# Zero products between the real ones on TensorE, a new order for the index work of slot 0, and small operations spread over more iterations, in a fused attention and two-expert-layer kernel

## The chip, the cores and the metric

The kernel runs on one core of one Trainium2 chip. The metric is the device time of one execution in microseconds (us), the median over the runs shown. The profile is of one execution of its own, with its own time.

## What is computed

The reference is a windowed attention and, behind it, two mixture-of-experts layers. Sizes: batch 4, 8 heads, 576 positions, head size 64; then 2304 tokens of 512 values, 8 experts with 1024 hidden units. One expert is chosen for each token.

```python
scores = (q @ k.T) / sqrt(64)               # heads 0-3: the last 32 positions
scores = where(mask, scores, -1e9)          # heads 4-7: every 4th of the last 128
x = softmax(scores) @ v                     # -> x: [2304, 512]
...
logits = x @ w_gate;  e = argmax(logits)    # layer 1
out[e==i] = gate * sigmoid(x @ w_output_gate)[:, i] * (relu(x @ w1[i]) @ w2[i])
...
logits = x @ w_gate + modality_bias[modality]   # layer 2, on layer 1's output
out[e==i] = gate * (relu(x @ w1[i]) @ w2[i])
```

## The kernel before

The core has TensorE (PE, its weight loads shown as PEld), VectorE (DVE), ScalarE (ACT), GpSimd (POOL) and SyncE (SP, which issues most DMAs). Each engine takes its instructions strictly in the order in which the program issues them (`tc.manual_schedule()`), so the order of the calls in the source is the order on each engine.

**Attention.** There are 16 pairs of heads, n = 0 to 15 (`NPR`). For pair n the stages are: `khi`, `klo`, `qsc`, `qsplit`, `qdup` split q and k into two half-precision parts on ACT, DVE and POOL; `stA(n, g)` (lines 388 to 399) makes the scores of group g (three groups) on PE and takes their row maxima on DVE; `stM` (from line 401) turns the maxima into a small bias on POOL (six operations, lines 415 to 420; the last pair's on DVE); `stMT` (line 430) transposes it on PE and ACT copies it out; `stB` (lines 443 to 446) makes the transposed scores on PE and their exponential on ACT; `stC(n, h)` (line 459) multiplies by v on PE, and behind h = 1 DVE normalises in three operations (lines 463 to 466); `stH` and `stZ` (474, 481) split the result into two parts on ACT and POOL (DVE for the last two pairs) and write it to `x_dram` through SP; `stX` (514, 521) transposes the last pairs' x on PE; `stR` (530, 531) makes the router's logits `lg1`. The function `iteration(n)` runs these for different pairs in the order of the list `ORDER`:

```python
ORDER = 'C0 T A0 H DV S0 Q0 Z A1 MT Q1 P0 S1 C1 K0 W L0 B0 X0 A2 D X1 K1 DW R S2 L1 B1 B2 P1 DQ MS'.split()
STEP = {'A': (stA, 1), 'B': (stB, 0), 'C': (stC, -1), 'X': (stX, -2), ...}
```

The number beside a stage is its offset: A works on pair n+1, C on n-1. At the place `W`, which lies behind C1 and ahead of L0, and at the start of the iteration, generators are stepped: `first_expert` (`fes`, from iteration 8) finds from the first 512 tokens the expert that will have the first slots; its result `gi` is read by SP at `DW` of iteration 10, where the loads of that expert's weights begin (two pieces of 512 KB in each of iterations 10 to 13). At iteration 3 `slot_consts` (12 small DVE operations, lines 153 to 164) and `token_values` (one, line 170) run in one go. `tail()` writes out by hand the order of what is left behind iteration 14, with `his` and `los` (splitting the loaded weights into a high part on ACT, line 102, and a low part on DVE, line 107) and `fs` (the steps of `first_slots`) between the stages.

**Expert layers.** Tokens are sorted by expert and worked through in slots of 128. `first_slots` picks the tokens of slots 0 and 1 (`KA` = 2) by itself: maxima, ranks by two products on PE (250, 251), one-hot rows `A` (line 230), products that give the token numbers (275), the numbers as integers (278), two gathers by POOL from `x_dram` (280), and a transposition on PE for each slot (`turn`, 542, 543). `sort` does the same for all tokens: step 1 maxima and one-hot (724 to 739), step 2 products (743 to 746), step 3 places (750 to 824), step 4 the one-hot matrix `A` (230), step 5 products (834), step 6 the integer indices (838), the gathers of slots 2 to 4 (903), a `table` of the experts (787 to 815) and the load of slot 3's weights by `start.weights(KE)` (line 94, on SP, 8 pieces), step 7 and 8 the gates (848 to 875), step 9 their products (880).

`moe` runs slot after slot. A slot is: `mm1(0)` and `mm1(1)` (line 940, 48 products of 128 columns each, `ph`), each followed by `hsplit` (ReLU and high part on ACT, line 950; low part `hl` on DVE, line 951), then 24 products of 512 columns into `py` (line 1012). Slots 0 to 2 use the weights loaded during attention, slot 3 the first that the table names; `first_splits(FIRST[i])` splits a quarter of these on ACT and DVE. Work is put into a slot by `at(s, k, ...)`: k = 0 start, 8 and 1 in `mm1(0)` behind 8 and 32 products, 2 behind it, 3 ahead of `mm1(1)`, 4 in it behind 32, 5 behind the second `hsplit`, 9, 6 and 10 behind 4, 12 and 20 products into `py`, 7 the end. `post.out` scales a slot's result on ACT and DVE (1155, 1156), `post.turn` transposes it (1174, 1175), `post.router` makes layer 2's logits (1183, 1192) in a PSUM tile `plg`. Slots from `NMIN` = 18 on stand in nested `tc.If(nsl > s)` (line 1041), with a branch hint for PE and DVE (`HINT`). Layer 2 runs through the same code with `so2`, `start2` and its own list of `at` (lines 1297 to 1312); its last slot of layer 1 is finished inside its slot 0 (`post1.out(None, ...)`, 1151 to 1153).

## Time and profile before

| | us |
|---|---|
| three runs | 639.43, 640.17, 644.14 |
| median | 640.17 |
| the profiled execution, its own time | 638.38 |
| its span, first to last instruction | 636.6 |
| PE busy | 589.1 (93% of the span) |
| DVE, ACT, POOL busy | 359.9, 272.8, 196.1 |
| attention with its tail, to the first product of slot 0 | 0 to 150.6 |
| layer 1, layer 2 | 150.6 to 419, 419.9 to 627.7 |

A row of the timeline gives the start and the length in us, the engine, the line, the operation, the tile written and the tiles read with their sizes, and how many instructions the row stands for. In brackets stands how long the engine had been idle, and whose work ended that. The granted clock is the share of 2.4 GHz that TensorE was given: 1.00 is 2.4 GHz, 0.50 is 1.2 GHz.

### The profile page before, as it was taken

What the parts mean: (1) busy time and instruction counts of PE and PEld (TensorE: products, weight loads), DVE (VectorE), ACT (ScalarE), POOL (GpSimd) and SP (SyncE); (2) the same over time, 40 slices, a digit from 0 to 9 for tenths busy, and PEclk for the clock granted to TensorE, in tenths of its full rate; (3) what the DMA queues carried; (4) which work ended last, traced back from release to release, by engine and by line L of the source; (5) the groups of instructions that cost most, each with busy time, mean ns of one, the idle gap of its engine ahead of it and who ended that gap; (6) DMA issues with size and microseconds to landing.
All of it is one profiled execution on the core that took longest, in us unless ns stands there. A gap on an engine that the chain in (4) does not pass through costs nothing. (4 is left out here: it accounts for less than half of the span.)

```text
span 636.6 us, 19375 instructions
## 1 busy us (share of the span) xinstructions
PE 589.1 (93%) x7380; PEld 456.1 (72%) x7380; DVE 359.9 (57%) x657; ACT 272.8 (43%) x370; POOL 196.1 (31%) x307
## 2 busy tenths in 40 slices
PE   3888889977999999999999999989999999999994
PEld 2868778867668677687776777856777777777772
DVE  6798898888889327944859732247530101013560
ACT  5677767773294126823538411110632111114550
POOL 2567767613151310111110610002654221212120
PEclk9799989975999999999999999999999999999998
DMA  8766668972499856996968683301994423233921
GB/s 290 243 191 194 211 198 273 293 167 72 146 357 368 226 117 180 378 243 151 266 198 221 169 153 65 69 21 36 324 323 121 99 60 93 63 91 114 300 56 37
DMA packets 100864, 114.15 MB, mean 179 GB/s; under 512 B 64399, under 2 KB 69263, under 8 KB 100752
## 3 DMA queue, kind: packets, MB, share of 16 engines
q1 hardware_dynamic: 95072, 94.89, 52.5%
q0 software_dynamic: 5280, 17.13, 9.1%
q8 instruction: 59, 0.97, 0.6%
q10 hardware_dynamic: 400, 0.72, 0.3%
q14 instruction: 53, 0.43, 0.2%
HBM read 209.13 MB, written 18.22 MB: 357 GB/s over the span
## 5 line engine op out<-in xcount | busy, mean ns | idle before, releaser
L940 PEld LDWEIGHTS <-wb 128*128 128x128 f16 x4032 | 229.7, 98 | 7.3 <-issue 1.5
L940 PE MATMUL ph<-xT,wb 128*128 128x128 f16 x3648 | 210.5, 219 | 1.1 <-ACT xT L919 1.1
L951 DVE SCALAR_TENSOR_TENSOR hl<-ph,hh 128x512 f16<-128x512 f32 x84 | 57.7, 689 | 162.8 <-ACTq L959 152.8
L1012 PE MATMUL py<-wb,hh 128*128 128x512 f16 x608 | 137.8, 379 | 0.0
L950 ACT ACTIVATE hh<-ph 128x512 f16<-128x512 f32 x84 | 50.2, 597 | 147.7 <-PE ph L940 147.3
L1012 PEld LDWEIGHTS <-hh 128*128 128x128 f16 x672 | 63.6, 98 | 68.0 <-ACT hh L950 0.3
L107 DVE SCALAR_TENSOR_TENSOR wb<-raw,wb 128x1024 f16<-128x1024 f32 (+1 forms) x80 | 104.7, 1346 | 12.7 <-ACT wb L102 11.3
L102 ACT ACTIVATE wb<-raw 128x1024 f16<-128x1024 f32 (+1 forms) x80 | 87.2, 1135 | 8.2 <-issue 2.8
L1012 PE MATMUL py<-wb,hl 128*128 128x512 f16 x304 | 72.0, 379 | 0.4 <-issue 0.4
L1012 PEld LDWEIGHTS <-hl 128*128 128x128 f16 x336 | 32.9, 98 | 40.2 <-issue 0.7
L1286 POOL DMA_INDIRECT out<-y,idx x16 | 16.2, 1010 | 98.9 <-ACTq L959 80.8
L459 PE MATMUL po<-v,pT 128*96 128x65 f32 x384 | 40.7, 258 | 0.1
L459 PEld LDWEIGHTS po<-v,pT 128*96 128x96 f32 x384 | 37.6, 174 | 0.2 <-DVE xh L466 0.2
L398 PE MATMUL ps<-kk,qs 128*96 128x128 f16 x192 | 30.0, 229 | 4.5 <-DVE qs L382 2.2
L398 PE MATMUL ps<-kk,ql 128*96 128x128 f16 x192 | 30.1, 230 | 4.2 <-DVE ql L376 4.2
L1285 ACT ACTIVATE y<-py,gsb 128x512 f32<-128x512 f32 x16 | 11.0, 687 | 52.3 <-PE py L1012 52.3
L399 DVE TENSOR_REDUCE M<-ps 96x4 f32<-96x512 f32 x48 | 31.6, 681 | 2.6 <-PE ps L398 2.0
L903 POOL DMA_INDIRECT xg<-x_dram,idxaa x23 | 24.4, 1061 | 27.6 <-DMA xT<-xg 18.0
L398 PEld LDWEIGHTS <-ql 128*96 128x96 f16 x192 | 23.5, 130 | 12.5 <-DVE ql L376 5.9
L446 ACT ACTIVATE pT<-pst 128x384 f32<-128x384 f32 x48 | 23.5, 489 | 20.4 <-PE pst L445 19.7
L443 PE MATMUL pst<-mt,msel 128*128 128x96 bf16 x192 | 29.9, 216 | 2.4 <-ACT mt L432 2.4
L398 PEld LDWEIGHTS <-qs 128*96 128x96 f16 x192 | 23.9, 130 | 8.8 <-issue 3.2
(407 smaller groups left out, 726.2 us busy)
## 6 DMA issues: line engine op xcount, KB each, us to landing
raw<-in_w1a SPq DMA_DIRECT2D x95, 512.0 KB
raw<-in_w2a SPq DMA_DIRECT2D x92, 512.0 KB
raw<-in_w1b SPq DMA_DIRECT2D x75, 512.0 KB
raw<-in_w2b SPq DMA_DIRECT2D x72, 512.0 KB
qk<-in_qk SPq DMA_DIRECT2D x16, 608.0 KB
v<-in_vw SPq DMA_DIRECT2D x16, 390.0 KB
y_dram<-y SPq DMA_DIRECT2D x11, 260.0 KB
y_dram<-lotmp SPq DMA_DIRECT2D x10, 260.0 KB
```

The costliest lines, as they stand in the source:

```text
L102: nc.scalar.activation(wb[:, 0, s], raw[:, s], AF.Copy, scale=SW)
L107: nc.vector.scalar_tensor_tensor(out=wb[:, 1, s], in0=raw[:, s], scalar=SW, in1=wb[:, 0, s], op0=ALU.mult, op1=ALU.subtract)
L398: nc.tensor.matmul(ps[:, j, :], q[:, h, QT * i:QT * i + QT], kk[:, h, QT * i:QT * i + 128], start=False, stop=w == 1 and j == 3, skip_grou ...
L399: nc.vector.tensor_reduce(out=Ms[n][:, 4 * g:4 * g + 4], in_=ps, axis=AX.X, op=ALU.max)
L443: nc.tensor.matmul(ps[:, j, :], msel[:, typ, j, :], mt[:, g, :], start=j == 0, stop=False, skip_group_check=True)
L446: nc.scalar.activation(pTs[n][:, 4 * g:4 * g + 4, :], ps, AF.Exp, scale=0.125 / (SQK * SQK))
L459: nc.tensor.matmul(po[:, h, i, :], pT[:, NQ * h + i, :], v[:, h, i, :], start=True, stop=True)
L903: nc.gpsimd.indirect_dma_start(t, None, src, bass.IndirectOffsetOnAxis(start.idx[:, s:s + 1], 0))
L940: nc.tensor.matmul(ph[:, j, :], w[:, c, fs], xT[:, parts[c + i], :], start=k == 0, stop=k == 47, skip_group_check=True)
L950: nc.scalar.activation(hs, ph, AF.Relu)
L951: nc.vector.scalar_tensor_tensor(out=hl[:, 4 * g:4 * g + 4, :], in0=ph, scalar=0.0, in1=hs, op0=ALU.max, op1=ALU.subtract)
L1012: nc.tensor.matmul(to, a, w, start=k == 0, stop=k == len(ops) - 1)
```

## The change

Zero products: a helper `warm` multiplies the zero tile `zt` with itself, 512 columns at a time, into a PSUM tile that nobody reads. It is called at the head (14 at the start, then 7, 6, 2 and 2) and at nine places of `tail()` (29 products in all, six of them inside `stX`). `slot_consts` is cut into four parts that run in iterations 0 (two), 1 and 2, `token_values` moves to `W` of iteration 3. `first_expert` gets more steps, so that `gi` comes at `W` of iteration 10 instead of 9, and one of its operations moves to POOL. In the tail, the last pair's `stC(b, 1)` comes ahead of `stX(a, 1)`, and its normalisation behind the last index step of `first_slots`. The sort of layer 1 runs at other hooks, the first splits' last quarter one hook later, layer 2's indices and gathers five hooks earlier than its table. One router product gets another PSUM tile and an earlier place, and DVE no longer gets branch hints.

```diff
@@ -37,7 +37,6 @@
 NSP = 28
-HINT = [mybir.EngineType.PE, mybir.EngineType.DVE]
 TOK0 = 1536.0
@@ -153,12 +152,15 @@
         v.tensor_scalar(si, si, 1, None, op0=ALU.logical_shift_right)
+        yield
         v.tensor_copy(s_odd, so)
...
         v.tensor_scalar(s_even, s_odd, -1.0, 1.0, op0=ALU.mult, op1=ALU.add)
+        yield
         v.tensor_tensor(s_even, s_even, s_half, op=ALU.mult)
...
         v.tensor_scalar(s_half, s_half, KA - 1.0, None, op0=ALU.add)
+        yield
         v.tensor_scalar(s_two, iota_t, 2.0, None, op0=ALU.mult)
@@ -183,14 +185,21 @@
         mx, eq, mi, me, cnt = T("mx", [P, n]), T("eq", sh), T("mi", [P, n]), T("me", [P, E]), T("cnt", [P, E], F16)
+        t = gp if nm == "a" else v
         v.tensor_reduce(out=mx, in_=lg0, axis=AX.X, op=ALU.max)
         v.tensor_tensor(eq, lg0, mx.unsqueeze(2).to_broadcast(sh), op=ALU.is_equal)
-        v.tensor_tensor(eq, eq, desc.unsqueeze(1).to_broadcast(sh), op=ALU.mult)
+        t.tensor_tensor(eq, eq, desc.unsqueeze(1).to_broadcast(sh), op=ALU.mult)
+        if nm == "a":
+            yield
         v.tensor_reduce(out=mi, in_=eq, axis=AX.X, op=ALU.max)
         v.tensor_tensor(eq, eq, mi.unsqueeze(2).to_broadcast(sh), op=ALU.is_equal)
+        if nm == "a":
+            yield
         v.tensor_reduce(out=me, in_=eq.rearrange("p t e -> p e t"), axis=AX.X, op=ALU.add)
...
         yield
+        if nm == "a":
+            yield
         pm = psum()
@@ -199,7 +208,8 @@
         v.tensor_reduce(out=m, in_=me, axis=AX.X, op=ALU.max)
-        yield
+        if nm != "a":
+            yield
@@ -385,6 +395,12 @@
+        WP = (14, 7, 6, 2, 2)
+
+        def warm(ps, k):
+            for i in range(k):
+                nc.tensor.matmul(ps, zt[:, 0:P], zt[:, 0:512], start=True, stop=True)
+
         def stA(n, g):
@@ -392,6 +408,8 @@
             nc.tensor.matmul(ps, identb[:QT, :QT], mS[kind][:, 4 * g:4 * g + 4, :], start=True, stop=False, skip_group_check=True)
+            if g == 0 and n < 2:
+                warm(wps, WP[1 + n])
             for j in range(4):
@@ -425,6 +443,8 @@
                 return
+            if n == 0:
+                warm(wps, WP[3])
             pm = ps_x.tile([P, 3, QT], BF16, name="pm", tag="px")
@@ -434,6 +454,8 @@
             kk, mt = kks[n], mts[n]
+            if g == 0 and n == 0:
+                warm(wps, WP[4])
             if g == 0:
@@ -457,8 +479,14 @@
                 nc.tensor.matmul(po[:, h, i, :], pT[:, NQ * h + i, :], v[:, h, i, :], start=True, stop=True)
-            if h == 0:
+            if h == 0 or n == NPR - 1:
                 return
+            normalise(n)
+
+        def normalise(n):
+            b, hp = divmod(n, 4)
+            xh = x_half[b, hp // 2]
+            po = pos[n][:, :, 0:65 * NQ].rearrange("q h (i c) -> q h i c", c=65)
             rc = ap2.tile([QT, 2, NQ, 1], F32, name="rc")
@@ -502,7 +530,7 @@
-        def stX(n, g):
+        def stX(n, g, wpt=None):
             if n // 2 in FL['dt']:
@@ -510,6 +538,8 @@
             for w in range(2):
+                if w and wpt is not None:
+                    warm(wpt, 3)
                 for i in range(3):
@@ -562,6 +592,7 @@
             a, b = NPR - 2, NPR - 1
+            wpt = ps_s.tile([P, 512], F32, name="wpt", tag="ps")
             his(2, 3)
@@ -570,6 +601,7 @@
             stZ(b - 2)
+            warm(wpt, 6)
             stB(b, 0)
@@ -585,20 +617,27 @@
             stC(b, 0)
+            warm(wpt, 3)
             fs()
-            stX(a, 0)
-            stX(a, 1)
+            stX(a, 0, wpt)
             fs()
             stC(b, 1)
+            warm(wpt, 2)
+            stX(a, 1)
+            warm(wpt, 2)
             fs()
+            fs()
+            normalise(b)
             stH(b)
-            fs()
             stR(a - 2)
+            warm(wpt, 3)
             stR(b - 2)
...
             los(4)
-            stX(b, 0)
+            warm(wpt, 2)
+            stX(b, 0, wpt)
             stX(b, 1)
+            warm(wpt, 5)
             stR(a)
@@ -621,12 +660,16 @@
                 nc.gpsimd.tensor_copy(midf, midt[:, :, 0])
-                slot_consts()
-                token_values()
+            if n == 0:
+                next(scs)
             if n >= fe_:
...
                 if o == 'W':
+                    if 0 <= n < 3:
+                        next(scs, None)
+                    if n == 3:
+                        token_values()
                     if n >= fe_:
@@ -663,6 +706,9 @@
         actx.enter_context(tc.manual_schedule())
+        scs = slot_consts()
+        wps = ps_v.tile([P, 2, 512], F32, name="wps", tag="po")[:, 0, :]
+        warm(wps, WP[0])
         for n in range(-4, NPR - 1):
@@ -840,6 +886,7 @@
             start.gather(i)
+        yield
         table()
@@ -976,7 +1023,7 @@
             if NMIN - 1 <= s < NSLOT - 1:
-                tc.mark_branch_hint_location(f"{start.name}{s + 1}", hint=nsl > s + 1, engines=HINT)
+                tc.mark_branch_hint_location(f"{start.name}{s + 1}", hint=nsl > s + 1, engines=PE)
             if s >= KE:
@@ -1002,6 +1049,8 @@
                 post.turn(s - 1)
+            if s == NMIN - 1:
+                post.router(s - 2, "pw")
             hook(5)
@@ -1013,8 +1062,6 @@
                     hook(9)
-                    if s == NMIN - 1:
-                        post.router(s - 2)
                 if k == 12:
@@ -1174,8 +1221,8 @@
-        def router(self, s):
-            pl = pp.tile([P, E], F32, name="plg", tag="plg")
+        def router(self, s, tag="plg"):
+            pl = pp.tile([P, E], F32, name=tag, tag=tag)
             yT = self.yT[0 if s is None else s % 2]
@@ -1213,10 +1260,9 @@
     at(0, 0, run(so1), lambda: lo_piece(wbuf[0], 12))
-    at(0, 1, run(so1, 2))
-    at(0, 2, run(fss))
-    at(0, 5, run(so1), lambda: lo_piece(wbuf[0], 14))
-    at(0, 10, run(so1, 2))
+    at(0, 3, run(so1), lambda: lo_piece(wbuf[0], 14))
+    at(0, 5, run(so1, 2), run(fss))
+    at(1, 1, run(so1, 3))
     at(1, 3, run(so1), start1.consts)
@@ -1225,11 +1271,10 @@
     at(2, 3, lambda: start1.first_splits(FIRST[2]))
-    at(2, 5, lambda: start1.first_splits(FIRST[3]))
     for i in range(NSLOT - NMIN):
...
     at(2, 5, first_out(post1, start1, 0))
-    at(2, 6, first_out(post1, start1, 1))
+    at(2, 6, first_out(post1, start1, 1), lambda: start1.first_splits(FIRST[3]))
     at(2, 7, lambda: post1.turn(0), lambda: post1.turn(1, "pw"), lambda: start1.part(KE + 1, *EARLY))
@@ -1289,7 +1334,7 @@
-        def router(self, s):
+        def router(self, s, tag=None):
             pass
@@ -1300,8 +1345,9 @@
     at(0, 7, run(so2, 2))
-    at(1, 9, run(so2, 2))
-    at(1, 7, lambda: start2.turned(KA))
+    at(1, 4, run(so2, 2))
+    at(1, 9, run(so2))
+    at(1, 10, lambda: start2.turned(KA))
     at(2, 2, lambda: start2.turned(KA + 1))
```

## Rows read from the trace of the kernel before

**Rows 1.** The page, part 2: granted clock, 40 slices, in tenths

```profile
PEclk9799989975999999999999999999999999999998
```

**Rows 2.** Windows; length, PE PEld DVE ACT POOL busy, clock, DMA share, GB/s

```profile
16.30:23.20 6.90, 5.93 (x61) 5.42 (x59) 4.40 (x7) 3.32 (x6) 3.61 (x7) 0.51 0.85 268
...
139.30:156.20 16.90, 12.76 (x165) 12.20 (x165) 13.44 (x36) 5.38 (x5) 4.65 (x12) 0.50 0.31 85
156.20:630.00 473.80, 465.49 (x5601) 344.63 (x5598) 229.84 (x397) 169.51 (x227) 108.86 (x154) 1.00 0.60 169
```

**Rows 3.** Timeline, DVE, line 463, five of sixteen; idle time in brackets

```profile
33.39 0.17 DVE L463 TENSOR_SCALAR rc<-po 96x12 f32<-96x12 f32 x1 [0.98 <-PE po L459]
...
42.58 0.16 DVE L463 TENSOR_SCALAR rc<-po 96x12 f32<-96x12 f32 x1
...
71.16 0.17 DVE L463 TENSOR_SCALAR rc<-po 96x12 f32<-96x12 f32 x1 [1.10 <-PE po L459]
...
81.49 0.16 DVE L463 TENSOR_SCALAR rc<-po 96x12 f32<-96x12 f32 x1
...
88.70 0.17 DVE L463 TENSOR_SCALAR rc<-po 96x12 f32<-96x12 f32 x1 [0.42 <-PE po L459]
```

**Rows 4.** Timeline, PE, DVE and POOL, attention's head

```profile
6.97 0.59 PE L394 MATMUL ps<-mS,identb 96*96 96x512 bf16 x1 [6.97 <-DMA mS<-in_cbs]
...
20.43 0.69 DVE L399 TENSOR_REDUCE M<-ps 96x4 f32<-96x512 f32 x1 [0.56 <-PE ps L398]
...
23.76 0.19 POOL L420 CAST mb<-r 96x12 bf16<-96x12 f32 x1
...
25.04 0.29 PE L430 MATMUL pm<-identb,mb 96*128 96x96 bf16 x3
```

**Rows 5.** Timeline, DVE and PE, first-expert work of iteration 8

```profile
77.07 1.63 DVE L188 TENSOR_TENSOR fe_eqa<-fe_eqa,cft 128x32 f32<-128x32 f32 x1
...
80.44 0.18 PE L195 MATMUL pfe<-fe_cnta,c16t 128*128 128x8 f16 x1 [2.13 <-DVE fe_cnta L192]
```

**Rows 6.** Timeline, DVE and PE, attention's tail, start of slot 0

```profile
140.29 1.02 DVE L230 TENSOR_TENSOR fs_A<-c16t,fs_fp 128x1664 f16<-128x1664 f16 x1
142.65 0.17 DVE L463 TENSOR_SCALAR rc<-po 96x12 f32<-96x12 f32 x1 [1.34 <-PE po L459]
...
150.98 0.30 DVE L724 TENSOR_REDUCE mxa<-lg 128x18 f32<-128x144 f32 x1 [0.85 <-DMA x_dram<-x]
...
150.56 3.57 PE L940 MATMUL ph<-xsA,wb 128*128 128x128 f16 x32 [0.71 <-ACT xsA L543]
```

**Rows 7.** Timeline, DVE, SP, ACT and PE, slots 0 to 3

```profile
162.22 1.21 DVE L107 SCALAR_TENSOR_TENSOR wb<-raw,wb 128x1024 f16<-128x1024 f32 x1
164.24 0.18 DVE L838 TENSOR_SCALAR idxaa<-pidx 128x27 int32<-128x27 f32 x1 [0.80 <-PE pidx L834]
...
168.71 1.98 SPq L94 DMA_DIRECT2D raw<-in_w1a  x4
...
181.14 0.61 ACT L950 ACTIVATE hh<-ph 128x512 f16<-128x512 f32 x1
...
182.82 3.62 PE L1012 MATMUL py<-wb,hh 128*128 128x512 f16 x16
...
189.67 0.40 PE L1174 MATMUL pyt<-identh,y 128*128 128x128 f16 x4 [0.70 <-DVE y L1156]
...
190.65 2.84 PE L940 MATMUL ph<-xT,wb 128*128 128x128 f16 x48
```

**Rows 8.** Timeline of PE and DVE, and line 1041's branches, both expert stages

```profile
362.14 0.44 PE L1183 MATMUL plg<-wr2h,yT 128*128 128x8 f16 x12 [0.86 <-DVE lg L1192]
...
422.40 0.75 DVE L1152 SCALAR_TENSOR_TENSOR y<-py,prg,y 128x512 f16<-128x512 f32 x1 [3.07 <-issue]
...
L1041 DVEq COMPARE_BRANCH  x10: 43/50/88, 362.6 to 625.8; - x10
...
446.56 2.84 PE L940 MATMUL ph<-xT,wb 128*128 128x128 f16 x48 [1.10 <-ACT xT L919]
```

## The prediction

> **What bounds the kernel now.** I read the granted clock first, over the whole span and then in windows. In the page's line of slices the reader is to see that the clock is below full only in the first 160 us (each slice is 15.9 us long) [rows 1]. The windows give the size: from 16.3 to 23.2 us the clock is 0.51 and PE works 5.93 us; from 139.3 to 156.2 us it is 0.50; behind that it is 1.00 to the end, and PE is busy for 465.5 of 473.8 us [rows 2]. So from the middle of slot 0 on the kernel is a full PE at full clock: whatever brings PE's stream forward there reaches the end one for one, and nothing else does.
>
> Second, the attention by the start of the normalisations on DVE. One iteration takes 88.70 - 81.49 = 7.21 us, but two take 42.58 - 33.39 = 9.19 and 81.49 - 71.16 = 10.33 us [rows 3]. The reader is to see that in normal iterations DVE waits for PE's `po` ahead of the normalisation (0.42 to 1.10 us), and in the two long ones it doesn't [rows 3]: there DVE itself is late, with one-off work.
>
> Third, single rows of the timeline for the head, the tail, slots 0 to 3 and the places behind them where PE waits.
>
> **Head.** Behind the clock's fall at 16.3 us DVE waits 0.56 us for the scores of pair 1, so pair 1's maxima, and POOL's bias that follows from them, come 0.56 us late. The bias is ready at 23.76 + 0.19 = 23.95, but PE transposes it only at 25.04 with no idle time: another 1.09 us [rows 4]. At full clock both go: 0.56 + 1.09 = 1.65 us. More than half of PE's 5.93 us [rows 2], 3.0, can't be had, and nothing if the clock falls in spite of the zeros: 0 to 3.0, and I take 1.65.
>
> The price of a zero product of 512 columns is that of a product into `py`, 3.62 / 16 = 0.23 us [rows 7], and twice that at half clock. PE's first real product waits until 6.97 us for its mask [rows 4]; 14 zeros cost 3.2 us at full and 6.3 us at half clock and are hidden by that wait. The other 17 stand ahead of products that wait for DVE, POOL or ACT; without that cover they would cost 17 x 0.23 = 3.9 us. I take nothing, with 1 us for the range.
>
> **Iterations 3 and 8.** The excess is 9.19 - 7.21 = 1.98 and 10.33 - 7.21 = 3.12, together 5.1 us. In iteration 8 the chain is seen on PE, which waits 2.13 us for the product of `first_expert` [rows 5]; the new steps put this product two iterations' worth of calls later, behind data that is long ready.
>
> What comes instead: of the cut operations, those stepped at the start of an iteration lie ahead of DVE's wait for `po`, and that wait hides them. Those stepped at `W` lie between the normalisation and the second half of the next split and maxima, and this stretch is on the loop (normalise, split, maxima, bias on POOL, transpose, `po`, normalise). At `W` stand three operations in iteration 1, three in 2, one in 3, two in 8 and four in 10 (`m` and the three ahead of it): 13. One such small operation takes 0.17 us [rows 3], some 0.2 with its gap: 13 x 0.2 = 2.6 us, if all are on the path. What is left is 5.1 - 2.6 = 2.5 us. Best is 5.1, if all 13 are hidden; worst, if two of them are blocked for 1.63 us each as the one in iteration 8 was [rows 5], 2.5 - 3.3 = -0.8.
>
> The multiplication at 77.07 takes 1.63 us on 32 elements, where a small one takes 0.17 [rows 5, 3]: something held it. The Trainium skill, SBUF — State Buffer, section "Who interferes with whom", states that a VectorE instruction with two SBUF inputs and a GpSimd instruction that reads SBUF exclude each other for their whole length. The trace agrees with such a block by this length. By the rule alone every moved operation with two SBUF inputs that meets POOL's split work would be held again, and the gain here would be nearer to the -0.8 than to the 2.5.
>
> SP reads `gi` ahead of the first weight loads, and q, k and v loads are queued behind that. `gi` now comes at `W` of the same iteration. No row prices this wait: between 0 and one iteration's excess as seen in iteration 8, 3.1 us; I take 0, since SP's place `DW` is behind `W`, and keep 1 us of it in the range.
>
> **Tail.** The one-hot matrix of slots 0 and 1 is ready at 140.29 + 1.02 = 141.31; DVE then waits 1.34 us for `po` and normalises at 142.65 [rows 6]. With `stC(b, 1)` ahead of `stX(a, 1)` that wait is gone; next comes the index (13 small products, some 0.45 us after the 0.44 of twelve in rows 8, and itself, 0.2), and the normalisation starts at about 142.05, 0.6 us earlier. What follows (split, write to `x_dram`, logits) moves with it. Sort's first operation at 150.98 waits for that write [rows 6], so DVE starts slot 0 at 150.4, again 0.6 earlier. PE reaches slot 0 at 150.56 behind ACT's copy of the turned tokens [rows 6]; the index no longer lies behind the normalisation, so the gather is issued some 2 us earlier, the copies ahead of it come 0.6 earlier, and eight transpositions at full clock (four take 0.40 [rows 7]) save another 0.4: about 149.5, 1.05 earlier. The 29 zeros (6.7 us at full clock) stand in front of products that wait; up to 1 us of them may show.
>
> **Slots 0 to 2.** PE's work up to 156.2 us at half clock [rows 2] would give back half of 156.2 - 150.56, 2.8 us. Does it arrive? DVE works without a gap from 150.98 to 162.22 + 1.21 = 163.43 [rows 6, 7]: sort, two low parts of weights, two `hl`. The new order puts all of that ahead of the index products, and lets the second `hl` wait some 0.65 us for PE: the list ends at 163.43 - 0.6 + 0.65 = 163.5. Before, the last low part lay behind the one-hot matrix, and the index came at 164.24 [rows 7]. So the index, the gathers, the table and the load of slot 3's weights at 168.71 stay within 0.5 us where they were. In slot 2 ACT splits those weights as they land and only then does `hh`, at 181.14 [rows 7]; PE's products into `py` started at 182.82 because PE was there no earlier. Now PE is there 3 us earlier and waits for `hh`: start at 181.14 + 0.61 + 0.3 = 182.05, 0.8 earlier. From there `out` ahead of the last quarter's split takes away the 0.70 us wait ahead of slot 3 [rows 7]. Slot 3 starts 0.8 + 0.7 = 1.5 us earlier than 190.65. Bounds: all of PE's own gain, 1.05 + 2.8 + 0.7 = 4.6; or, if the index comes 1 us later than before, 0.5. The clock's gain in slot 0 is thus mostly handed on to a wait for `hh`.
>
> **Behind that.** In slot 17 PE waits 0.86 us for DVE to free `plg` [rows 8]; with `pw` I take 0.85 (0 to 0.86). In layer 2 PE waits 1.10 us for the turned tokens of slot 2 [rows 8]; indices and gathers come 16 products of 128 columns and 4 of 512 earlier, 16 x 0.06 + 4 x 0.23 = 1.9 us [rows 7]; I take 0.8 (0 to 1.1), as the turned tokens then wait for their place in PE's stream.
>
> **Sum.** 1.65 + 2.5 + 1.5 + 0.85 + 0.8 = 7.3 us off the profiled execution's 638.38 (span 636.6): 631.1. The runs' median, 640.17, is 1.8 above this execution, and the lowest run, 639.43, 1.0 above. With the lowest run's offset the forecast is **632.1**.
>
> **Rivals.**
> 1. *PE's gain arrives whole in slots 0 to 3*, since ACT meets landed weights: 4.6 instead of 1.5, 629.0. For it: PE is at half clock there. Against: `hh` at 181.14 follows the splits. Chance 0.15.
> 2. *The clock isn't held*: the zeros are fewer than the waits. Then 1.65 is lost, and zeros cost 0.45 each where they show, 1 us: 634.8. For it: between the real products of the tail PE waits for copies. Chance 0.12.
> 3. *The index of the first expert comes too late*: loads behind SP's read slip, later weight pieces land later, and 3 us are given back: 635.1. For it: SP is one queue. Against: the later pieces are issued iterations later anyway. Chance 0.13.
> 4. *Slower: DVE's branches without hints.* At the change of layers DVE has 3.07 us in which the profile shows nothing it waits for, with a hint; line 1041 has 10 branches on DVE [rows 8]. If each, unhinted, costs such a stop, the ceiling is 30.7 us. DVE has cover in these slots; the case decides at 7.3 / 10 = 0.73 us uncovered for each. At half of each uncovered, 15.4 - 7.3 = 8 over before: 648.3. Against: ACT and POOL pass the same line unhinted. Chance 0.05. The Trainium skill, Runtime: NRT & Kernel Launch, section "Instruction fetch mechanics", states that a taken branch to code outside the fetched pages stops the engine for a fetch. The 3.07 us fit it, even with a hint; no row here shows an unhinted DVE.
>
> **How the numbers follow.** The forecast has 0.55, the rivals 0.45. The range: up to rivals 2 and 3 with their zeros' and SP's us, 637.0; down to rival 1 with three quarters of what iterations 3 and 8 could give beyond 2.5 us, 627.0. One per cent, about what can be told from no change, is 633.8. Four fifths of the forecast's chance, rival 1 and a little of 2 and 3 lie below: 0.62. Rival 4 is 0.05, 0.33 is between.
>
> **What would show it.** Right: clock 1.00 from about 9 us; normalisations 7.2 to 7.8 us apart throughout; first product of slot 0 some 5 us earlier; `idxaa` 14 us or more behind it; in slot 2 PE waits for `hh`; no wait for `plg`. Wrong: a clock of 0.5 in the tail; a normalisation 9 us behind the last; PE without a wait in slot 2; DVE idle for over 3 us in gated slots with PE behind it.

## The result and the profile after

The changed kernel takes 632.62 us (median of four runs, 631.73 to 633.55) beside 640.36 us for the kernel before in the same session (639.43 to 644.14): a ratio of 0.9872, 95% interval 0.9844 to 0.9900. A second session on another chip gave 633.27 beside 640.96 us, 0.9887 (0.9867 to 0.9906). The forecast was 632.1 us. The total agrees to half a microsecond; its parts do not all agree, and that is what this section and the experiments are about.

The page of the changed kernel, part 2, shows one of the first ten slices with the clock below full, where the kernel before has four [rows 1] (the last slice, where the work ends, is below full in both):

```profile
PEclk9999998999999999999999999999999999999998
```

The windows (columns as in rows 2) show where this is: the head, the tail and the first 10 us of slot 0 run at the full clock, and the only stretch at half clock ahead of the last product is a new one, at 98 us.

```profile
16.30:23.20 6.90, 6.32 (x86) 4.84 (x84) 6.35 (x13) 4.70 (x7) 4.09 (x11) 1.00 0.87 270
98.00:101.00 3.00, 3.00 (x26) 2.77 (x26) 1.33 (x3) 1.89 (x3) 2.70 (x3) 0.50 1.03 356
...
139.00:148.00 9.00, 6.50 (x101) 4.44 (x100) 7.12 (x13) 3.28 (x3) 3.13 (x12) 1.00 0.42 126
148.00:158.00 10.00, 10.00 (x115) 7.17 (x113) 8.39 (x26) 2.10 (x3) 1.41 (x5) 1.00 0.01 2
```

The normalisations on DVE answer to rows 3. Each row's start is to be compared with the row above it.

```profile
32.05 0.17 DVE L491 TENSOR_SCALAR rc<-po 96x12 f32<-96x12 f32 x1 [0.98 <-PE po L481]
39.37 0.17 DVE L491 TENSOR_SCALAR rc<-po 96x12 f32<-96x12 f32 x1 [1.10 <-PE po L481]
...
68.14 0.17 DVE L491 TENSOR_SCALAR rc<-po 96x12 f32<-96x12 f32 x1 [1.10 <-PE po L481]
75.32 0.17 DVE L491 TENSOR_SCALAR rc<-po 96x12 f32<-96x12 f32 x1
83.09 0.17 DVE L491 TENSOR_SCALAR rc<-po 96x12 f32<-96x12 f32 x1 [0.76 <-PE po L481]
90.39 0.17 DVE L491 TENSOR_SCALAR rc<-po 96x12 f32<-96x12 f32 x1 [0.48 <-PE po L481]
99.60 0.17 DVE L491 TENSOR_SCALAR rc<-po 96x12 f32<-96x12 f32 x1 [2.02 <-PE po L481]
```

The stretches of 9.19 and 10.33 us [rows 3] are gone: 39.37 - 32.05 = 7.32 and 75.32 - 68.14 = 7.18. What follows iteration 8's normalisation takes 7.77, and what follows iteration 10's takes 99.60 - 90.39 = 9.21. (In the experiments "iteration n" is counted like that, from its own normalisation to the next one.) The rows of DVE, POOL and PE behind 90.39 show the chain of that long one:

```profile
91.73 0.15 DVE L207 TENSOR_REDUCE fe_m0a<-pfe 128x1 f32<-128x8 f32 x1
92.51 0.79 DVE L366 SCALAR_TENSOR_TENSOR kk<-qk,kk 64x608 f16<-64x608 f32 x1
94.62 0.64 POOL L220 TENSOR_TENSOR fe_oa<-fe_oa,fe_ua 128x8 f32<-128x8 f32 x1
95.23 0.86 POOL L433 TENSOR_SCALAR r<-M 96x12 f32<-96x12 f32 x1
97.50 0.30 PE L450 MATMUL pm<-identb,mb 96*128 96x96 bf16 x3 [1.10 <-POOL mb L438]
```

The four small DVE operations of `m` push the split `kk` back by 92.51 - 91.73 = 0.78 us; POOL's five operations with the result end at 94.62 + 0.64 = 95.26, and only then comes the bias; PE waits 1.10 for it, and the clock falls.

The tail, on PE, DVE and POOL, and PE's first product of slot 0:

```profile
139.14 0.52 PE L560 MATMUL pl<-wr1h,xT 128*128 128x16 f16 x15
139.42 0.23 DVE L561 TENSOR_TENSOR lg<-pl,lg 128x80 f32<-128x80 f32 x1
141.34 0.24 DVE L561 TENSOR_TENSOR lg<-pl,lg 128x80 f32<-128x80 f32 x1 [1.69 <-remote]
...
140.94 0.33 POOL L291 TENSOR_SCALAR ea_cons<-fs_r 128x13 f32<-128x13 f32 x1
...
142.50 0.56 PE L544 MATMUL px<-identh,x 96*128 96x96 f16 x9 [1.13 <-DVE x L509]
146.69 0.49 PE L987 MATMUL ph<-xsA,wb 128*128 128x128 f16 x6 [0.74 <-ACT xsA L573]
```

DVE stands for 1.69 us between two additions of logits; `remote` says that the view names no instruction that ended this wait. The second addition reads what PE's products at 139.14 write, and those end, as modelled, at 139.66. The trace also records when semaphores go up: the one of PE that this addition waits for goes up at 141.32, 0.02 us ahead of DVE's start. In layer2_old, a run without the stop, the same semaphore goes up at 138.77, 0.02 us behind the end of these products. So DVE waited for PE's signal, and the signal came 1.65 us late. The paragraph on pace below and the run cons_first come back to it. The split behind the stop comes late, and PE waits 1.13.

Slots 0 to 2 and the places behind them (DVE, SP, PE, ACT), to be held against rows 7 and 8:

```profile
160.40 0.18 DVE L884 TENSOR_SCALAR idxaa<-pidx 128x27 int32<-128x27 f32 x1 [0.48 <-PE pidx L880]
165.19 1.71 SPq L93 DMA_DIRECT2D raw<-in_w1a  x4
183.05 1.02 PE L1061 MATMUL py<-wb,hl 128*128 128x512 f16 x4 [0.71 <-POOL y L1196]
...
351.06 0.45 PE L1230 MATMUL pw<-wr2h,yT 128*128 128x8 f16 x12
415.14 0.75 DVE L1199 SCALAR_TENSOR_TENSOR y<-py,prg,y 128x512 f16<-128x512 f32 x1 [1.29 <-ACT y L1198]
438.97 1.22 PE L987 MATMUL ph<-xT,wb 128*128 128x128 f16 x19 [0.24 <-ACT xT L966]
455.17 1.91 ACT L101 ACTIVATE wb<-raw 128x2048 f16<-128x2048 f32 x1 [1.88 <-DMA raw<-in_w2b]
458.48 1.90 PE L1061 MATMUL py<-wb,hh 128*128 128x512 f16 x8 [1.67 <-ACTq L1006]
```

The index comes 160.40 - 146.69 = 13.71 us behind the first product of slot 0, as before (164.24 - 150.56 = 13.68). The wait of 0.86 us for `plg` is gone, and so is DVE's stop of 3.07 us with no wait shown. In layer 2 the wait ahead of slot 2 falls from 1.10 to 0.24, and a new one of 1.67 us stands in slot 3, behind weights that landed late. In slot 2 of layer 1 PE now stops 0.71 us ahead of the last four products into `py`, where it also loads the slot count; 0.42 stood there before.

By stretches, from the starts of such rows (us). Normalisations are counted by pair, so pair 13's is the 14th. "Same pace" is explained below; it is the changed kernel but for two small POOL operations in the tail (the run cons_first).

| stretch | before | after, gain | second profile, gain | same pace, gain | forecast |
|---|---|---|---|---|---|
| start to first normalisation | 26.40 | 1.74 | 1.55 | 1.87 | 1.65 |
| to pair 13's normalisation | 98.81 | 2.13 | 3.05 | 3.07 | 2.5 |
| to slot 0 | 25.35 | 0.00 | 0.02 | 0.35 | 1.05 |
| slot 0 to slot 4 | 51.71 | 1.14 | 0.66 | 0.28 | 0.45 |
| slot 4 to layer 2 | 217.59 | 0.53 | 0.11 | 1.08 | 0.85 |
| layer 2 to the last product | 207.82 | -0.70 | -0.19 | 2.20 | 0.8 |
| sum | 627.68 | 4.84 | 5.20 | 8.85 | 7.3 |

The two profiles of the changed kernel show 5 us, the medians 7.7. The profile of before seems to stem from a chip of a quicker pace (its chip isn't known): its gated slots in layer 2 take 10.54 us each, as in the kernels profiled on the chip where before's medians were 638.35 and 638.22 us, while both profiles of the changed kernel have slots of 10.5 to 11.1 and stand beside medians of 640.4 and 641.0. The slower pace goes with PE's signals: in both profiles of the changed kernel, and in the other four of chips of this pace, 35 to 39 of PE's some 507 signals come late or aren't found beside the end of their product, in before and in the seven profiles of the quicker chip 1 to 3. The stop in the tail is one of these. At its own pace, the profiles of m_now, layer2_old and cons_first, which differ little from the changed kernel, end 7.4, 8.5 and 8.9 us earlier.

### The profile page after: what moved, and what is told of

The parts are those of the page before. It is cut to its first block, busy times and chain, and to the rows that moved or that the text cites. A ratio compares the mean times of both kernels' runs of the same rounds, so it can differ in the third digit from the quotient of the medians.

```text
span 631.8 us, 19474 instructions
## 1 busy us (share of the span) xinstructions
PE 595.4 (94%) x7440; PEld 451.0 (71%) x7440; DVE 356.0 (56%) x656; ACT 273.1 (43%) x370; POOL 193.5 (31%) x308
## 5 line engine op out<-in xcount | busy, mean ns | idle before, releaser
L987 PEld LDWEIGHTS <-wb 128*128 128x128 f16 x4032 | 227.4, 98 | 7.9 <-issue 1.4
L101 ACT ACTIVATE wb<-raw 128x1024 f16<-128x1024 f32 (+1 forms) x80 | 87.5, 1135 | 13.8 <-DMA raw<-in_w2a 3.1
L481 PE MATMUL po<-v,pT 128*96 128x65 f32 x384 | 39.1, 252 | 0.6 <-PE pst L467 0.6
L481 PEld LDWEIGHTS po<-v,pT 128*96 128x96 f32 x384 | 35.8, 167 | 1.4 <-issue 0.7
L950 POOL DMA_INDIRECT xg<-x_dram,idxaa x23 | 26.0, 1131 | 26.0 <-DMA xT<-xg 18.0
L416 PE MATMUL ps<-kk,ql 128*96 128x128 f16 x192 | 28.6, 222 | 4.4 <-DVE ql L386 4.3
L416 PE MATMUL ps<-kk,qs 128*96 128x128 f16 x192 | 28.6, 222 | 3.9 <-DVE qs L392 2.7
L416 PEld LDWEIGHTS <-ql 128*96 128x96 f16 x192 | 22.2, 124 | 11.2 <-DVE ql L386 6.3
L1239 DVE SCALAR_TENSOR_TENSOR lg<-plg,lg 128x8 f32<-128x8 f32 x21 | 3.5, 165 | 45.3 <-PE plg L1230 44.7
L465 PE MATMUL pst<-mt,msel 128*128 128x96 bf16 x192 | 27.5, 207 | 0.6 <-ACT mt L452 0.6
```

The costliest lines, as they stand in the source:

```text
L101: nc.scalar.activation(wb[:, 0, s], raw[:, s], AF.Copy, scale=SW)
L416: nc.tensor.matmul(ps[:, j, :], q[:, h, QT * i:QT * i + QT], kk[:, h, QT * i:QT * i + 128], start=False, stop=w == 1 and j == 3, skip_grou ...
L465: nc.tensor.matmul(ps[:, j, :], msel[:, typ, j, :], mt[:, g, :], start=j == 0, stop=False, skip_group_check=True)
L481: nc.tensor.matmul(po[:, h, i, :], pT[:, NQ * h + i, :], v[:, h, i, :], start=True, stop=True)
L950: nc.gpsimd.indirect_dma_start(t, None, src, bass.IndirectOffsetOnAxis(start.idx[:, s:s + 1], 0))
L987: nc.tensor.matmul(ph[:, j, :], w[:, c, fs], xT[:, parts[c + i], :], start=k == 0, stop=k == 47, skip_group_check=True)
```

## The experiments

Each run gives a ratio to the kernel before on its own chip, and one profile.

**The kernel again.** No edit.

> The changed kernel once more, unchanged. Theory: two places of its first profiled execution are chance and not the kernel's: the 9.21 us of iteration 10 with the clock at 0.5 behind it, and the 1.69 us that DVE waited ahead of the logits in the tail. In a second profile iteration 10 takes 8.5 us, slot 0 starts near 144.6 instead of 146.69, and the time against the kernel before is 0.987 to 0.988. Rival: both belong to the change; they are there again, and slot 0 starts near 146.7.

0.9887 (0.9867 to 0.9906). Iteration 10 took 8.49 us, without a fall of the clock, so 0.7 of the 9.21 was chance. The stop in the tail was there again, so that half of the theory falls. It came back in all four profiles of this chip, each time with PE's signal 1.6 to 1.7 us behind the modelled end of its products:

```profile
138.69 0.23 DVE L561 TENSOR_TENSOR lg<-pl,lg 128x80 f32<-128x80 f32 x1
140.58 0.24 DVE L561 TENSOR_TENSOR lg<-pl,lg 128x80 f32<-128x80 f32 x1 [1.66 <-remote]
...
140.23 0.32 POOL L291 TENSOR_SCALAR ea_cons<-fs_r 128x13 f32<-128x13 f32 x1
```

**Without the zeros.**

```diff
-            for i in range(k):
+            for i in range(0):
                 nc.tensor.matmul(ps, zt[:, 0:P], zt[:, 0:512], start=True, stop=True)
```

> All products of zeros are left out of the changed kernel (they only write a scratch bank, so nothing that is computed goes missing). Theory, each part pays in its own place: the clock falls again in iterations 0 and 1 of the attention and the 1.74 us of the head go; in the tail PE runs at half clock, but DVE and ACT set the end there, so the stretch from the normalisation of iteration 13 to the first product of slot 0 stays at its 17.15 us within 0.5; slot 0 is slower by some 3 us at half clock, of which about two thirds were handed on to later waits anyway. Sum 1.7 + 1.3 = 3.0 us: 635.6. Rival A, the clock is held by the other changes: 632.6 and a clock of 1.00 behind 9 us. Rival B, all that slot 0 gained reaches the end: 1.7 + 3.2 = 4.9 us, 637.5.

0.9947 (0.9928 to 0.9966): 634.59 beside 638.35 us, so the changed kernel's gain halves. Windows of this run, tail and slot 0:

```profile
139.00:148.00 9.00, 5.03 (x98) 4.47 (x99) 7.60 (x15) 3.95 (x4) 4.99 (x12) 0.61 0.44 124
148.00:158.00 10.00, 10.00 (x118) 8.54 (x117) 6.81 (x18) 2.10 (x3) 0.11 (x1) 0.84 0.01 2
```

Against layer2_old, on the same chip: the first normalisation comes 26.03 - 24.76 = 1.3 us later, the stretch from pair 13's normalisation to slot 0 takes 25.28 instead of 24.23, and slot 0 to slot 4 takes 53.50 instead of 51.51. At slot 4 the loss is 201.10 - 196.19 = 4.9 us. That is rival B: what slot 0 gains by the clock arrives at slot 4, and of the 4.9 us the medians of this chip show 4.3 to 4.5 (634.59 beside 630.07 for layer2_old and 630.32 for cons_first).

**The zeros alone,** in the kernel before.

```diff
+        wps = ps_v.tile([P, 2, 512], F32, name="wps", tag="po")[:, 0, :]
+        warm(wps, WP[0])
         for n in range(-4, NPR - 1):
...
             stZ(b - 2)
+            warm(wpt, 6)
             stB(b, 0)
```

> The kernel before with the products of zeros alone, at the same places of head and tail, nothing else changed. Theory: with the old order of slots 0 and 1 the clock's gain there is handed on (the changed kernel with that order back took 51.1 us from slot 0 to slot 4, the kernel before 51.7 with half clock), so the zeros are worth the head's 1.7, about 1.0 in the tail and 0.6 in slots 0 to 3: 3.3 us, a ratio of 0.995. Rival: the clock is worth the same 4.9 to 5.8 us at slot 4 that the changed kernel loses without its zeros: 0.992.

0.9973 (0.9957 to 0.9990): less than either expected, 1.7 us in the medians of 12 runs. The profile is the fastest of them (634.55 us) and shows the expected terms: head 26.40 - 24.61 = 1.79, tail 25.35 - 24.21 = 1.14, slots 0 to 3 51.71 - 50.98 = 0.73. The twelve runs' mean clocks go from 0.984 to 0.995 (0.988 to 0.997 in the nine of the changed kernel), and the slowest runs are among those of the lowest clocks: the zeros don't hold the clock in every execution. How much of what is missing from the expected 3.3 us this explains isn't shown.

**Order of slots 0 to 2 put back.**

```diff
-    at(0, 3, run(so1), lambda: lo_piece(wbuf[0], 14))
-    at(0, 5, run(so1, 2), run(fss))
-    at(1, 1, run(so1, 3))
+    at(0, 1, run(so1, 2))
+    at(0, 2, run(fss))
+    at(0, 5, run(so1), lambda: lo_piece(wbuf[0], 14))
+    at(0, 10, run(so1, 3))
...
-    at(2, 6, first_out(post1, start1, 1), lambda: start1.first_splits(FIRST[3]))
+    at(2, 6, first_out(post1, start1, 1))
```

> In the changed kernel the order of the index work in slots 0 and 1 and the place of the last quarter's split in slot 2 are put back. Theory of the prediction: the index, the gathers and slot 3's weights hang on DVE's list, which is as long in either order, so the index comes 13.7 us behind the start of slot 0 again, and only the wait of 0.70 us ahead of slot 3 returns: 0.7 us slower than the changed kernel. Rival: the new order is what lets slots 0 and 1 use the full clock (DVE's hl no longer stands behind index work), and slot 1 starts 1 us or more later without it: 1.7 us slower or more.

0.9914 (0.9894 to 0.9933), 635.25 beside 633.27 us for after_again, with intervals that overlap. The profile, the fastest of its six runs, shows no loss: slot 0 to slot 4 takes 197.45 - 146.37 = 51.08 us, 51.05 in after_again. Slot 0 is 2.0 us longer, and slots 1 to 3 are 1.3, 0.2 and 0.5 us shorter. Taken together for slots 0 to 3 (us):

| | half clock in the first 3.6 to 5.6 us of slot 0 | full clock |
|---|---|---|
| old order | 51.71 (before) | 50.98, 51.08 |
| new order | 53.50 (no_zeros) | 50.57 to 51.51 (nine profiles, without best_e, whose slot 1 is edited) |

The new order doesn't pay by itself, and at half clock it costs 1.8 us; it ties the index to PE, since `hl` of slot 0 now stands ahead of it on DVE: the index comes 13.72 us behind the start of slot 0 in after_again and 15.42 in no_zeros. The expected 13.7 us for the old order is missed, too: there the index came at 12.49, and nothing of that reached slot 4. That the median of slots_old is 2 us longer isn't explained by its profile and stays open.

**One-off work put back** (`slot_consts`, `token_values` and `first_expert` in one go).

```diff
-        t = gp if nm == "a" else v
+        t = v
...
-            if n == 0:
-                next(scs)
...
+                list(scs)
+                token_values()
```

> In the changed kernel the constants of the slots, the values of the tokens and the first expert's chain are put back as before, in one go in iterations 3 and 8. Theory: iteration 3 loses 1.5 us and iteration 8 some 3.0, and iteration 10, which in the changed kernel takes 9.21 us with four small operations behind the normalisation, returns to 7.2: 4.5 - 2.0 = 2.5 us net, 635.1, with the first product of slot 0 later by as much. Rival: iteration 10 is long for another reason (the read of the first expert's index by SP, the loads behind it) and stays at 9.2: 4.5 us net, 637.1.

0.9927 (0.9908 to 0.9945). The long stretches are back with 9.17 and 10.32 us, and iteration 10 takes 7.24: the theory. From the first normalisation to pair 13's it takes 98.75 - 95.69 = 3.06 us longer than layer2_old. A further 1.1 us of this run's profile were lost at 136 to 140 us, where the clock was 0.68.

**DVE's branch hints put back.**

```diff
-                tc.mark_branch_hint_location(f"{start.name}{s + 1}", hint=nsl > s + 1, engines=PE)
+                tc.mark_branch_hint_location(f"{start.name}{s + 1}", hint=nsl > s + 1, engines=[mybir.EngineType.PE, mybir.EngineType.DVE])
```

> The branch hints of DVE are put back into the changed kernel, nothing else. Theory: the hint made the stop of 3.07 us on DVE at the change of layers, with no wait shown; it comes back, PE waits 1.17 us again behind it in slot 0 of layer 2, and the slots 3 to 17 of layer 1 and 3 to 17 of layer 2 stay within 0.3 us: 632.6 + 1.2 = 633.8. Rival: the stop came from where the code stood, not from the hint; it does not return: 632.6.

0.9921 (0.9902 to 0.9940). The stop and PE's wait behind it are there again (DVE and PE, start of layer 2):

```profile
414.51 0.75 DVE L1199 SCALAR_TENSOR_TENSOR y<-py,prg,y 128x512 f16<-128x512 f32 x1 [3.12 <-issue]
...
415.32 0.40 PE L1221 MATMUL pyt<-identh,y 128*128 128x128 f16 x4 [1.23 <-DVE y L1199]
```

Slot 0 of layer 2 takes 13.83 us, 12.43 in layer2_old on the same chip. The hint made the stop; without it PE gains 1.2 us at this place. What DVE does in the stop isn't shown.

**Layer 2's order put back.**

```diff
-    at(1, 4, run(so2, 2))
-    at(1, 9, run(so2))
-    at(1, 10, lambda: start2.turned(KA))
+    at(1, 9, run(so2, 3))
+    at(1, 7, lambda: start2.turned(KA))
```

> In the changed kernel the order of layer 2's index work is put back: index, gathers, table and the next weights' load together at hook 9 of slot 1, the turned tokens of slot 2 at hook 7. Theory: the earlier gathers and transposed loads run into the load of slot 3's weights, whose last piece then came 1.67 us late for PE. Put back, PE waits some 0.85 us more ahead of slot 2 and no longer 1.67 us in slot 3: 632.6 - 0.8 = 631.8. Rival: the late piece has nothing to do with the order (it is late in both): 632.6 + 0.85 = 633.4.

0.9873 (0.9854 to 0.9891), the changed kernel's own ratio. PE waits 1.10 us ahead of slot 2 again, and not in slot 3 (PE):

```profile
438.07 2.11 PE L987 MATMUL ph<-xT,wb 128*128 128x128 f16 x35 [1.10 <-ACT xT L966]
...
455.74 3.62 PE L1061 MATMUL py<-wb,hh 128*128 128x512 f16 x16
```

From layer 2's start to its slot 4 the old order took 48.21, 48.39 and 48.43 us in three profiles (best_a and best_b have it too). The new order, with the hints left out, took 47.35, 47.36, 48.36, 48.43, 48.47, 48.72 and 49.35: in five of seven PE waited 0.6 to 1.67 us in slot 3. On average nothing is won, 48.3 both. The late piece goes with the new order: none of the three profiles of the old one has it. What holds it up isn't shown.

**POOL's operations ahead of the gathers.**

```diff
-        for i in range(KA):
-            gp.indirect_dma_start(xg[i], None, src, bass.IndirectOffsetOnAxis(idx[:, i:i + 1], 0))
         gp.tensor_scalar(ea["cons"], r, float(KA * P), None, op0=ALU.is_lt)
         gp.tensor_tensor(ea["consr"], ea["cons"], r, op=ALU.mult)
+        for i in range(KA):
+            gp.indirect_dma_start(xg[i], None, src, bass.IndirectOffsetOnAxis(idx[:, i:i + 1], 0))
```

> In the changed kernel POOL's two small operations on 13 elements in the tail (L291, L292) are issued ahead of the two gathers instead of behind them. Theory: DVE's stop of 1.66 us ahead of the second logits in the tail has no semaphore; it ends at 140.58, where POOL's first small operation ends (140.23 + 0.32), so these two engines kept each other off. With POOL's operations earlier the stop goes and slot 0 starts 7.5 us behind the last normalisation, not 8.57: 1.1 us. Rival A: the gather itself, through at 140.20, holds DVE: the stop stays at 1.3 us or more. Rival B: the stop depends on the chip and not on this order: present or absent here whatever the order.

0.9882 (0.9866 to 0.9899). The stop isn't there, but this chip doesn't decide it: layer2_old, dve_hints, m_now, no_zeros and oneoff_old ran on it with the changed kernel's order and had none either. There PE's signal came on time, DVE went on, and POOL's operation, 0.33 us elsewhere, took 1.66 to 1.78. The rows of layer2_old show that it was held by DVE (DVE, then POOL): it ends at 141.70, 0.13 us behind the second of them.

```profile
139.48 0.95 DVE L509 TENSOR_TENSOR x<-xh,x 96x768 f16<-96x768 f32 x1 [0.40 <-ACT x L502]
140.36 1.21 DVE L106 SCALAR_TENSOR_TENSOR wb<-raw,wb 128x1024 f16<-128x1024 f32 x1
...
140.03 1.67 POOL L291 TENSOR_SCALAR ea_cons<-fs_r 128x13 f32<-128x13 f32 x1
```

So the theory that POOL and DVE kept each other off in the stop falls: DVE waited for PE there. Rival A fits none of this chip's profiles, in which the gather ran as well. Rival B fits: with the order unedited, the five profiles with the stop are the first one and all four of one chip, whose signals of PE come late in many places, and the five without it are all of this chip. Slot 0 starts 8.24 us behind the last normalisation since PE's `pl` waited 1.42 us for the DMA of `xT`.

**The operations of m at the start of iteration 10.**

```diff
         nc.tensor.matmul(pm, ones, cnt, start=True, stop=True)
-        yield
+        if nm != "a":
+            yield
         m, m0 = T("m", [P, 1]), T("m0", [P, 1])
...
-        if nm != "a":
-            yield
+        yield
```

> In the changed kernel the four small DVE operations that read the first expert's counts (m0 to m) are issued at the start of iteration 10, right behind the product; POOL's five stay at W. Theory: in iteration 10 these four stand 0.78 us in the loop on DVE, and POOL's five, which wait for them, end at 95.42 and hold the bias by another 1.2; at the start DVE has cover, so iteration 10 falls from 8.5 to 7.2 or 7.5 us: 1.0 to 1.3 us. Rival: POOL's five are the cost by themselves, and iteration 10 stays above 8.2: under 0.3 us.

0.9862 (0.9844 to 0.9880). Iteration 10 falls to 7.22, as expected, but iteration 9 rises to 8.66: there one of the four is blocked by POOL's subtraction (DVE, then POOL):

```profile
90.06 1.51 DVE L210 TENSOR_TENSOR fe_mea<-fe_mea,cft 128x8 f32<-128x8 f32 x1
...
89.91 1.64 POOL L509 TENSOR_TENSOR x<-xh,x 96x768 f16<-96x768 f32 x1
```

The two end together, at 91.57 and 91.55. Iterations 9 and 10 take 15.88 us, 15.79 in after_again: nothing won in this profile. It also shows a fall of the clock (0.78 at 80 to 84 us) with iteration 8 at 8.64 instead of 7.77, where nothing was edited. The rival falls: with POOL's five operations still at `W` iteration 10 is short.

**Two tries at a better kernel.** best_a issues the product and `m` half an iteration earlier and takes layer 2's old order; best_b also moves the gates behind the second split of slot 1:

```diff
-        if nm == "a":
-            yield
         pm = psum()
...
-    at(1, 3, run(so1), start1.consts)
-    at(1, 5, run(so1))
+    at(1, 5, run(so1), start1.consts, run(so1))
```

> Two edits to the changed kernel: the first expert's four small operations are issued at the start of iteration 10, ahead of DVE's wait for po, and its product one half iteration earlier; and layer 2's index work stands in its old order. Theory: iteration 10 falls from 8.5 to 7.2 us, 1.3 us; layer 2 loses 0.9 ahead of its slot 2 and gains 1.2 to 1.7 in slot 3: 1.3 + 0.6 = 1.9 us faster than the changed kernel. Rival: iteration 10 is long because of POOL's and SP's work with the index, which stays: 0.6 us.

> As best_a, and in slot 1 the gates' operations (dl to gate, with two exponentials on ACT) and the constants of the second router are issued behind the second split of the hidden values instead of ahead of it. Theory: PE's wait of 1.36 us for hh in slot 1 goes, but slot 2 ends behind slot 3's weights, whose load hangs on DVE's table and not on PE: slot 3 starts within 0.4 us of best_a's. Rival: PE's time arrives: 1.3 us faster than best_a.

0.9897 (0.9880 to 0.9915) and 0.9911 (0.9892 to 0.9931), beside after_again's 0.9887: no gain. Behind the earlier product PE waits 2.00 us for DVE's `lg` at 86.59 (both use the PSUM tag `px`), and iterations 8 to 10 take 24.4 us instead of 23.6; in best_b the clock fell there too (0.61 at 88 to 92 us), 26.3. Slot 0 to slot 4 takes 51.14 and 51.21: PE's wait for `hh` in slot 1 goes in best_b, and nothing reaches slot 4, as expected.

**Four edits together.**

```diff
-        v.tensor_tensor(me, pm, m0.to_broadcast([P, E]), op=ALU.is_equal)
-        v.tensor_tensor(me, me, desc, op=ALU.mult)
+        v.scalar_tensor_tensor(out=me, in0=pm, scalar=m0, in1=desc, op0=ALU.is_equal, op1=ALU.mult)
...
+            if 8 <= n <= 10:
+                for _ in range(3):
+                    nc.tensor.matmul(pmf, zt[:, 0:P], zt[:, 0:3 * QT], start=True, stop=True)
...
+            if i == 0:
+                gp.tensor_scalar(ea["cons"], r, float(KA * P), None, op0=ALU.is_lt)
...
+                if k == 4 and s == KE - 2:
+                    count()
```

> Four edits to the changed kernel, each from one of the runs before: (1) the first expert's operations on the counts at the start of iteration 10, with comparison and weighting as one operation that has only one operand beside PSUM; (2) three products of zeros of 288 columns ahead of the transposition of the bias in iterations 8 to 10; (3) POOL's two small operations of the tail between the two gathers; (4) PE's load of the slot count in slot 1, where PE waits 1.35 us for hh, instead of slot 2. Theory: iterations 8, 9 and 10 take 7.8, 7.3 and 7.3 us without a fall of the clock (22.4 together; the changed kernel took 23.6 and 24.3); slot 0 starts 7.5 to 7.8 us behind the last normalisation; the wait of 0.87 us in slot 2 goes. Sum about 2.5 us against the changed kernel, a ratio to the kernel before of 0.984. Rival: what is won before slot 3 is taken by the wait for slot 3's weights or by the last weight piece in layer 2, and the ratio stays at 0.987.

0.9880 (0.9858 to 0.9902): the rival. The first three edits did what they were to do. Iterations 8 to 10 take 7.54 + 7.67 + 7.23 = 22.44 us, slot 0 starts 7.50 us behind the last normalisation, and the fused operation takes 0.23 us. It begins 0.05 us ahead of POOL's subtraction, so it couldn't be held; the reduction behind it begins inside the subtraction and isn't held (DVE, POOL, then PE's first product of slot 0):

```profile
88.88 0.23 DVE L209 SCALAR_TENSOR_TENSOR fe_mea<-pfe,fe_m0a,cft 128x8 f32<-128x8 f32 x1
89.14 0.16 DVE L210 TENSOR_REDUCE fe_ma<-fe_mea 128x1 f32<-128x8 f32 x1
...
88.93 1.64 POOL L513 TENSOR_TENSOR x<-xh,x 96x768 f16<-96x768 f32 x1
...
144.17 2.00 PE L991 MATMUL ph<-xsA,wb 128*128 128x128 f16 x33 [0.74 <-ACT xsA L577]
```

Slot 0 starts 1.8 us earlier than in after_again, but slot 4 only 0.8: a wait for DVE's `hl` opens in slot 3, and in layer 2 the earlier count waits for the table (PE):

```profile
194.28 1.04 PE L1065 MATMUL py<-wb,hl 128*128 128x512 f16 x4 [0.95 <-DVE hl L1002]
...
434.27 2.10 PE L1065 MATMUL pya<-wb,hh 128*128 128x512 f16 x9 [1.43 <-DVE hnb L844]
```

In the tail DVE waits 0.27 us for PE's second `pl`, whose signal is 0.23 late; this profile is of a third chip, of the slower pace, and POOL's operations stand elsewhere, so it doesn't tell which of the two shortened the stop. No version here is measurably faster than the changed kernel.

## Why the prediction was right, and which steps were not

- **The bound and the clock** were right. With zeros the clock is 1.00 in head, tail and slot 0; without them it is not (0.61, 0.84), and the gain halves. Rival 2 falls.
- **Head**, forecast 1.65: 1.55 to 1.87 in three profiles, 1.3 lost without zeros.
- **Iterations 3 and 8**, forecast 2.5: 2.13, 3.05 and 3.07, and 3.06 by undoing. The excess was 5.1 as read. Iteration 9, 7.71 us before, falls to 7.30, a gain that the prediction didn't read. What came instead was mis-sized in its parts: behind iterations 1, 3 and 8 the operations at `W` cost 0.2 to 0.6 each time (7.39 and 7.17 where 6.99 stood, 7.77 where 7.21 stood), and the four of iteration 10 cost 1.3 us, 0.8 on DVE and the rest through POOL's five operations behind them, which the prediction didn't count.
- **Rival 3** (the index too late for SP's loads) is not seen: the normalisations behind iteration 10 are 7.2 to 7.4 us apart.
- **Tail**, forecast 1.05. The step "what follows moves with it" fails in five of the ten profiles that have this order: there DVE's stop of 1.7 us, a wait for a late signal of PE, takes all of it (0.00 and 0.02). Where the stop is absent the whole comes (25.35 - 24.23 = 1.12 in layer2_old, 24.26 in best_e).
- **Slots 0 to 2.** Index and loads stayed within 0.4 us of where the prediction left them (13.71 us behind slot 0 where 13.68 stood, 18.50 where 18.15 stood). The step that "PE now waits for `hh`" in slot 2 names the wrong place: PE lost most of its lead in slot 1 already, where it waits up to 1.36 us for `hh` behind ACT's exponentials. In slot 2 it doesn't wait for `hh` in the first profile, and 0.3 to 0.4 us in layer2_old, cons_first and m_now; the stop where it loads the slot count, 0.7 to 1.25 us, wasn't foreseen. Slot 3 starts 1.98 and 1.53 us earlier relative to pair 13's normalisation, where 1.5 was forecast, so that number was right by luck. Of this 0.85 us goes in slot 3 (11.62 us before, 12.46 and 12.47 after), 0.54 of it in a wait for DVE's `fe_cnt`. That the clock's gain is mostly handed on holds in the sum: slot 0 is 3.2 us shorter (14.35 to 11.13), and 0.2 to 1.1 are left at slot 4. But the new order itself costs 1.8 us there, which the prediction doesn't have, and in it the clock is worth 2.0 (53.50 - 51.51). Rival 1, 4.6 us at slot 3, falls.
- **The wait for `plg`**, forecast 0.85: gone in every profile with the change; 1.08 up to layer 2 at the same pace.
- **Layer 2's order**, forecast 0.8: the wait ahead of slot 2 went as forecast. What the prediction had not asked is what the earlier gathers may collide with: in five of seven profiles the last piece of slot 3's weights lands late and takes it back.
- **Rival 4** had the right place and the wrong sign. The stop of 3.07 us belonged to the hint. Taking it away is a gain of 1.2 us that no term of the sum holds; it fills the hole that layer 2's order leaves.

Three of the prediction's own signs went against it in the first profile: a normalisation 9.21 us behind the last, no wait for `hh` in slot 2, and the index 13.71 us behind slot 0 instead of 14 or more.

So the clock, the one-off work and `plg` were right in mechanism, and the total came as close as it did because errors cancel, which is luck: the tail (where PE's signal came late) and layer 2's order gave less than forecast, the one-off work and the hints more.

## What to carry to other kernels

Zeros in an engine's gaps pay where the engine's next stretch is the path, and they pay more with an order that makes the rest of the chain wait for that engine; test both together, since the zeros alone gave 0.9973 and the order without them lost 1.8 us in its place. An operation of 0.2 us costs by where it stands: at the start of iteration 8, ahead of DVE's wait, two of DVE's and one of POOL's were free (7.18 us); behind such a wait, with work of another engine in tow, four cost 1.3 us; and ahead of the wait, but beside POOL's subtraction, one of them took 1.51. Compare stretches only between profiles of the same pace: two chips differ here by 2 to 3 us in 640, more than most of the parts.

## What the runs showed of the hardware

- A branch hint can cost: with hints on DVE a stop of 3.07, 3.09 and 3.12 us at the change of layers in three profiles, without them none in eleven, in which slot 0 of layer 2 takes 12.4 to 12.6 us and not 13.8.
- DVE and POOL can keep each other off, in both directions. A DVE multiplication of 8 columns with two operands in SBUF took 1.51 us and ended with POOL's subtraction; a reduction with one operand, begun inside that subtraction, took 0.16. A POOL operation on 13 columns, 0.33 us elsewhere, took 1.67 beside two DVE operations with two operands in SBUF. The Trainium skill, SBUF — State Buffer, section "Who interferes with whom", says that a VectorE instruction with two SBUF inputs and a GpSimd instruction that reads SBUF exclude each other, and that one with at most one SBUF input, outside the modes that use both of VectorE's ports, does not; these rows agree.
- A signal of PE can come late. In five profiles the semaphore behind the second products of `pl` goes up 1.62 to 1.67 us behind their modelled end, 0.23 in best_e, and 0.02 in layer2_old, dve_hints, m_now and oneoff_old. It isn't this place alone: in the six profiles of the slower pace 35 to 39 of PE's some 507 signals aren't found within 0.06 us of the modelled end, in the other eight 1 to 3. In the five profiles with the stop the signal also comes within 0.06 us of the end of POOL's first small operation behind the gathers, but on the quicker chip the same gathers ran without a late signal. What makes these signals late, and whether the products are late themselves, isn't shown.
- The clock falls in some executions of a stretch and not in others: code that nobody had edited ran with a fall at 80 to 84 us in m_now and at 98 us in the first profile, and without either in after_again. Beside profiles without one, a fall cost 0.6 to 1.1 us.
